# Exponentials split over two PSUM banks each, two projections split by weight halves, a last output piece of 96 columns, and a new timetable

## Chip, cores and metric

One core of a Trainium2 chip. The metric is the device time of one launch in microseconds. The kernel before takes 442.77 us, the median of three runs (442.43 to 443.47). The profiled execution that all rows below come from took 442.87 us; its span, from the first to the last recorded instruction, is 441.1 us, so 1.77 us lie around the span.

## The reference

A transformer block over 2048 tokens of width 576: a memory-augmented attention, then a feed-forward layer, both behind a layernorm and with a residual.

```python
x = A_x                                     # 2048 x 576, bf16
q, k, v = LN(x) @ wq, LN(x) @ wk, LN(x) @ wv  # 32 heads of 18, 4 segments of 512 tokens
for s in range(4):
    p = softmax(q_s k_s^T * 18**-0.5 + causal_mask)      # inside the segment
    a_mem = (phi(q_s) @ M) / (phi(q_s) . z + 1e-6)       # phi(t) = t + 1 if t > 0 else exp(t)
    o_s = g * a_mem + (1 - g) * (p @ v_s)                # g = sigmoid(beta), per head
    M, z = M + phi(k_s)^T v_s, z + sum(phi(k_s))
h = x + concat(o) @ wo
out = h + gelu(LN(h) @ w1 + b1) @ w2 + b2   # hidden width 4608
```

## The kernel before

The program is written as a graph of small steps. `add` makes one step: the engines that may run it and a cost, the function that emits the instructions, the steps it comes after, and the buffers it takes and uses. The order in which steps are emitted, and the engine of each, are not decided at build time: they stand in `TIMETABLE` (line 25), a table from a step's tag and name to a letter (p TensorE, a ScalarE, d VectorE, g GpSimd, s the DMA queue of SyncE) and a rank. `schedule` emits the steps by rank and gives each buffer a slot by a simple model of when slots come free. Each engine then runs its list in order and waits on semaphores for what its next instruction needs.

The tags of the steps: X layernorm and transposing of x, P projections, A attention, M the memory matrix, B output projection and second layernorm, C first and D second feed-forward matmul; the digit is the segment. So A0 is the attention of segment 0. Feed-forward work of one segment is mixed with attention of a later one.

- **PSUM.** `c_s` (line 618) has eight banks of 128 x 512 f32. A width-4 buffer is bank 0 to 3 or 4 to 7. Single-bank buffers prefer banks 4 to 7 where those are free (`pick`, line 357).
- **Scores and exponentials.** One attention step works on four heads: `score` (lines 1020 and 1184) writes four banks by matmuls of 32 rows that run side by side (one bank for each row group), one exponential on ScalarE (lines 1030 and 1192) reads all four banks, 128 x 2048, into `pt`, and masks follow on VectorE or GpSimd (lines 1040, 1043, 1201, 1203). There are 80 such steps, 20 of them in A0. `val` (lines 1059, 1214) multiplies `pt` with v by matmuls of 19 output columns that run side by side.
- **Projections.** `proj2` (line 855, matmuls in line 863) makes k and q of the first two token tiles: two halves of five matmuls of 288 columns, one step of ten. `proj_pair` (line 793) makes the other 60 products, in one of two forms that the ranks decide: where its two steps follow each other directly on TensorE they are emitted as ten matmuls of 128 rows (line 849, called the full form here); where something stands between them, as ten and eight matmuls of 64 rows that run in pairs (line 823, the split form), with a small `pass` memset (line 829) on VectorE or GpSimd between the two halves, for which the second half waits.
- **Layernorm.** `layernorm` (line 733) is two or three VectorE instructions for the statistics (744, 745), two on GpSimd for the root (748, 749), and the apply on VectorE (758 or 760).
- **First loads.** x of tile 0 and 1, then wk as two DMAs of half each, x of tile 2, wq as one DMA of 720 KB, x of tile 3, beta.
- **A0's q and k.** Those of the first 128 tokens are transposed on TensorE (`TQ`, line 906). Those of the others are written to DRAM (`qkd`, line 918) and read back by transposing DMAs (`flip`, line 656) into `qk` and, for tokens 256 to 511, into the tail of `w2_lo` (called w_lo in the profile).
- **The end.** D3 makes 128 x 288 outputs by 36 matmuls each (line 1413); VectorE adds the residual (line 1425), and DMAs write the rows. The last tile is written as two DMAs of half a row each.

Of the kernel before, what the change touches and what calls it, by code (L numbers as in the profile page):

```python
# [335 lines left out]
}  # L336
# [159 lines left out]
def kernel(  # L496
# [12 lines left out]
    P = 128  # L509
# [1065 lines left out]
```

## Time and profile before

| what | value |
|---|---|
| median of three runs | 442.77 us |
| the profiled execution: time, span | 442.87 us, 441.1 us |
| granted TensorE clock | 1.00 over the whole span |
| TensorE busy | 431.6 us, 98% |
| ScalarE, VectorE, GpSimd busy | 297.6, 287.2, 172.7 us |
| 80 exponentials of 128 x 2048 | 150.2 us of ScalarE, 1.88 us each |
| chain that ended last | TensorE 91%, VectorE 3%, ScalarE 2%, DMA 2% |
| first matmul, first projection, last matmul ends | 1.24, 6.93, 438.1 us |

Busy time is the union of an engine's instruction records; matmul ends are modelled, so a busy TensorE can still lose time between matmuls. The chain is read back from the last instruction: each piece is what released the next. Where a row has "idle before" in brackets, the engine stood still for so long, and the name is what ended it.

### The profile page before, as it was taken

Reading aid. Unit: us, or ns where it says so; the run is one execution under the profiler, and the core shown is the slowest. Engines: PE = TensorE matmul, PEld = TensorE weight load, DVE = VectorE, ACT = ScalarE, POOL = GpSimd, SP = SyncE. Lnnn points to the kernel's source line nnn. Section 1 sums busy time; section 2 is a strip of 40 time slices with the busy share of each in tenths; the row PEclk is TensorE's granted clock in tenths of the full one; section 3 lists DMA queues with packets and bytes.
Section 4 is the critical chain, followed back from the end, with each engine's and each line's share of the span. In section 5 each row is a group of like instructions: output and inputs, shape, how many; then the busy total and the mean of one; then the engine's idle time right before and its main releaser. Section 6 shows DMA issues by size and latency. Waiting matters only on the chain.

```text
span 441.1 us, 12208 instructions
## 1 busy us (share of the span) xinstructions
PE 431.6 (98%) x5142; PEld 276.4 (63%) x5142; DVE 287.2 (65%) x651; ACT 297.6 (67%) x270; POOL 172.7 (39%) x317
## 2 busy tenths in 40 slices
PE   7988999999999999999999999999999999999997
PEld 4765677666677677664445666654547775446775
DVE  5999999898878989768899877646875020100002
ACT  3898899999888797777999977653495001656000
POOL 4586678457655434361514576251112010000010
PEclk9999999999999999999999999999999999999999
DMA  6799999988999955981762437924554350650012
GB/s 230 212 235 250 279 294 273 260 196 257 253 226 248 345 119 165 197 222 55 178 194 53 87 106 230 260 57 135 163 192 163 74 129 1 223 180 1 1 28 81
DMA packets 79991, 75.61 MB, mean 171 GB/s; under 512 B 57664, under 2 KB 67264, under 8 KB 79936
## 3 DMA queue, kind: packets, MB, share of 16 engines
q1 hardware_dynamic: 79792, 74.74, 62.6%
q8 instruction: 40, 0.66, 0.6%
q14 instruction: 15, 0.12, 0.1%
q10 hardware_dynamic: 144, 0.09, 0.1%
HBM read 42.30 MB, written 18.87 MB: 139 GB/s over the span
## 4 chain that ended last, share of the span: by engine, by line
PE 91%; DVE 3%; ACT 2%; DMA 2%; issue 1%; POOL 1%; ACTq 0%; DVEq 0%; POOLq 0%
PE bank L1413 33%; PE bank L1326 24%; PE bank L823 8%; PE bank L1363 8%; PE bank L849 5%; PE bank L1188 4%; PE bank L1214 3%; DMA x<-in_A_x_dram 1%; ACT pt L1030 1%; PE bank L1027 1%; PE bank L1059 1%; PE bank L1159 1%; PE bank L953 1%; DMA xnd<-xn 1%; PE bank L772 0%
## 5 line engine op out<-in xcount | busy, mean ns | idle before, releaser
L1413 PEld LDWEIGHTS <-hT 128*128 128x128 bf16 x1152 | 110.0, 98 | 34.7 <-issue 7.2
L1192 ACT ACTIVATE pt<-bank 128x2048 bf16<-128x2048 f32 x60 | 112.6, 1876 | 27.1 <-PE bank L1188 23.6
L1326 PE MATMUL bank<-xreg,w1g 64*128 64x512 bf16 x972 | 107.8, 376 | 0.0
L1326 PEld LDWEIGHTS <-w1g 64*128 64x128 bf16 x972 | 46.6, 94 | 56.4 <-issue 2.9
L1413 PE MATMUL bank<-w_lo,hT 128*128 128x288 bf16 x576 | 77.7, 286 | 0.0
L1413 PE MATMUL bank<-w,hT 128*128 128x288 bf16 x576 | 77.6, 286 | 0.0
L1425 DVE TENSOR_TENSOR ot<-bank,hc 128x288 bf16<-128x288 f32 x32 | 13.8, 451 | 78.1 <-PE bank L1413 70.1
L1331 ACT ACTIVATE hT<-bank,b_col 128x512 bf16<-128x512 f32 x36 | 22.0, 691 | 47.7 <-PE bank L1326 47.5
L1203 POOL TENSOR_SCALAR_AFFINE_SELECT pt<-pt 128x512 bf16<-128x512 bf16 x56 | 38.5, 697 | 26.8 <-ACT pt L1192 26.5
L1341 DVE TENSOR_SCALAR hT<-bank,b_col 128x512 bf16<-128x512 f32 x45 | 32.4, 742 | 16.4 <-PE bank L1326 16.1
L1399 POOL TENSOR_TENSOR hc<-hc,b_bc 128x576 f32<-128x576 f32 x8 | 10.3, 1285 | 77.4 <-DVE ot L1425 59.5
L1030 ACT ACTIVATE pt<-bank 128x2048 bf16<-128x2048 f32 x20 | 37.6, 1879 | 2.6 <-PE bank L1027 1.8
L1363 PE MATMUL bank<-xreg,w1g 64*128 64x256 bf16 x648 | 38.6, 269 | 0.5 <-issue 0.5
L1363 PEld LDWEIGHTS <-w1g 64*128 64x128 bf16 x648 | 30.7, 94 | 6.3 <-issue 2.9
L1346 ACT ACTIVATE hT<-hT 128x8192 bf16<-128x8192 bf16 (+2 forms) x6 | 31.8, 5321 | 0.1
L1339 ACT ACTIVATE hT<-bank,b_col 128x512 bf16<-128x512 f32 x27 | 17.4, 685 | 20.5 <-PE bank L1326 20.4
L823 PE MATMUL bank<-hT,xreg 64*128 64x288 bf16 x414 | 29.1, 283 | 0.6 <-DVE MZacc L963 0.5
L849 PE MATMUL bank<-hT,xreg 128*128 128x288 bf16 x210 | 28.4, 286 | 0.2 <-DVE xreg L669 0.2
L823 PEld LDWEIGHTS <-xreg 64*128 64x128 bf16 x414 | 18.8, 94 | 8.6 <-issue 2.6
L1374 DVE TENSOR_TENSOR hT<-bank,b_col 128x512 bf16<-128x512 f32 x30 | 19.6, 680 | 7.1 <-PE bank L1363 6.9
L1188 PE MATMUL bank<-qk 32*128 32x512 bf16 (+3 forms) x384 | 23.8, 301 | 0.1
L849 PEld LDWEIGHTS <-xreg 128*128 128x128 bf16 x210 | 19.6, 98 | 6.8 <-issue 1.7
(121 smaller groups left out, 590.3 us busy)
## 6 DMA issues: line engine op xcount, KB each, us to landing
w1g<-in_B_w_dram SPq DMA_DIRECT2D x41, 576.0 KB, 5.0
qkd<-qk_pad SPq DMA_DIRECT2D x15, 512.0 KB, 4.1
hd<-h SPq DMA_DIRECT2D x16, 288.0 KB, 4.6
hc<-hd SPq DMA_DIRECT2D x16, 288.0 KB, 3.6
w_lo<-in_B_w_dram SPq DMA_DIRECT2D x3, 864.0 KB, 6.4
w<-in_B_w_dram SPq DMA_DIRECT2D x3, 864.0 KB, 7.9
xb<-in_A_x_dram SPq DMA_DIRECT2D x16, 144.0 KB, 3.7
x2d<-xn SPq DMA_DIRECT2D x14, 160.0 KB, 2.1
```

The lines of the kernel that those rows point to most:

```text
L823: return nc.tensor.matmul(out=cc[hf].t[:, 0:HALF], lhsT=xTb.t[r, k, ts], rhs=wt[r, hf, k, :], start=start, stop=stop, skip_group_check=True)
L849: nc.tensor.matmul(out=cc[hf].t[:, 0:HALF], lhsT=xTb.t[:, k, ts], rhs=wt[:, hf, k, :], start=(k == 0), stop=(k == KT - 1))
L1030: ex = add(ps, {"act": 1.88}, lambda e: nc.scalar.activation(out=pt.t[:], in_=st.t[:], func=ACT.Exp, scale=scale), [sc], pt, [st], table=" ...
L1188: nc.tensor.matmul(out=st.t[:, i, off:off + n_], lhsT=qk[rows, 1, kt * P:(kt + 1) * P], rhs=qk[rows, 0, kt * P:L], start=True, stop=True, ...
L1192: ex = add(ps, {"act": 1.88}, lambda e, st=st, pt=pt: nc.scalar.activation(out=pt.t[:], in_=st.t[:], func=ACT.Exp, scale=scale), [sc], pt, ...
L1203: nc.gpsimd.affine_select(out=blk, in_=blk, pattern=[[0, 4], [1, P]], compare_op=ALU.is_ge, fill=0.0, base=0, channel_multiplier=-1)
L1326: nc.tensor.matmul(out=cc[w].t[:], lhsT=w1.t[rows, k, q, :], rhs=x2T[s].t[rows, k, :], start=(k == 0), stop=(k == ND - 1))
L1331: ready_f[f + w] = [add(pf - 12, {"act": 0.68}, lambda e, f=f, w=w, cc=cc: nc.scalar.activation(out=hT[:, :, f + w, :], in_=cc[w].t[:].rea ...
L1341: nc.vector.tensor_scalar(out=dst, in0=src, scalar1=b, scalar2=None, op0=ALU.add)
L1346: ge = add(2.9, {"act": 0.42 * (f1 - f0) + 0.2}, lambda e, f0=f0, f1=f1: nc.scalar.activation(out=hT[:, :, f0:f1, :], in_=hT[:, :, f0:f1, ...
L1363: nc.tensor.matmul(out=cc[w].t[:, q * 2 * P:(q + 1) * 2 * P], lhsT=w1.t[rows, k, q, :], rhs=x2T[s].t[rows, k, ts], start=(k == 0), stop=(k ...
L1413: nc.tensor.matmul(out=c.t[:, 0:HALF], lhsT=hT[:, tl // 2, f, (tl % 2) * P:(tl % 2 + 1) * P], rhs=w2_c[ch][:, f - ch * WCH, hf * HALF:(hf ...
```

## The change

- **Exponentials.** `exp_of` makes two instructions of 128 x 1024 for each step; each reads a buffer of two banks, which comes free by itself. Masks come after both. A score's four matmuls write two such buffers. `pick` now prefers single banks whose neighbour is taken.
- **First projections.** wq comes as two DMAs of half each; k and q of tiles 0 and 1 become two steps of five matmuls, of which each waits for its weight half alone.
- **Last output half.** The last 288 columns become 192 and 96, each with its own sum, add and DMA.
- **Applies.** A layernorm apply may stand on GpSimd too.
- **Planner constants.** The DMA model (295e3 for 270e3, 1.8 for 1.6) and the order of ranks: all of `TIMETABLE` is new.

```diff
-        return min([i for i in ready if i >= self.home.pref] or ready or range(len(free)), key=lambda i: free[i])
+        return min([i for i in ready if free[i ^ 1] > t0] or ready or range(len(free)), key=lambda i: free[i])
...
-    c_s = Slots([banks_all[:, j, :] for j in range(8)], banks_all, 4)
+    c_s = Slots([banks_all[:, j, :] for j in range(8)], banks_all, 8)
...
-            return add(prio, {"dve": dcost}, apply, [a, b if centred is None else None] + list(extra), dst_buf, [sm, xsrc], name="apply")
+            return add(prio, {"dve": dcost} if centred is not None else {"dve": dcost, "pool": round(dcost + 0.2, 2)}, apply, [a, b if centred is None else None] + list(extra), dst_buf, [sm, xsrc], name="apply")
...
-                        w_ok["q"] = load_w(-7.4, "q", 0)
+                        w_ok["q"] = [load(-7.4 + 0.01 * h, lambda h=h: wts["q"][:, h, :, :].rearrange("p k d -> p (k d)"),
+                                          lambda h=h: A_w[0:P, h * KT * HALF:(h + 1) * KT * HALF], 350e3) for h in range(2)]
...
-            def fn(e):
-                for hf in range(2):
-                    for k in range(KT):
-                        nc.tensor.matmul(out=c.t[:, hf, 0:HALF], lhsT=xTb.t[:, k, ts], rhs=wt[:, hf, k, :],
-                                         start=(k == 0), stop=(k == 4))
-            return add(prio, {"pe": 1.24}, fn, list(after) + w_ok[nm], c, [xTb], name="P" + nm)
+            def fn(e, hf):
+                for k in range(KT):
+                    nc.tensor.matmul(out=c.t[:, hf, 0:HALF], lhsT=xTb.t[:, k, ts], rhs=wt[:, hf, k, :],
+                                     start=(k == 0), stop=(k == 4))
+            a = add(prio, {"pe": 0.62}, lambda e: fn(e, 0), list(after) + w_ok[nm][0:1], c, [xTb], name="P" + nm)
+            return add(prio, {"pe": 0.62}, lambda e: fn(e, 1), list(after) + [a] + w_ok[nm][1:2], None, [c, xTb], name="R" + nm)
...
+        def exp_of(prio, st, pt, sc):
+            ops = []
+            for j in range(2):
+                ops.append(add(prio, {"act": 1.04}, lambda e, j=j: nc.scalar.activation(out=pt.t[:, 2 * j:2 * j + 2, :], in_=st[j].t[:], func=ACT.Exp, scale=scale),
+                               [sc] + ops, [] if j else pt, [st[j]] + ([pt] if j else []), table="exp", name="exp"))
+            return ops
...
-                st, pt = Buf(c_s, width=4), Buf(pt_s)
+                st, pt = [Buf(c_s, width=2), Buf(c_s, width=2)], Buf(pt_s)
...
-                            nc.tensor.matmul(out=st.t[:, i, off:off + n_], lhsT=qk[rows, 1, kt * P:(kt + 1) * P],
+                            nc.tensor.matmul(out=st[i // 2].t[:, i % 2, off:off + n_], lhsT=qk[rows, 1, kt * P:(kt + 1) * P],
...
-                ex = add(ps, {"act": 1.88}, lambda e, st=st, pt=pt: nc.scalar.activation(out=pt.t[:], in_=st.t[:], func=ACT.Exp, scale=scale),
-                         [sc], pt, [st], table="exp", name="exp")
-                exps.append(ex)
+                ex = exp_of(ps, st, pt, sc)
+                exps.extend(ex)
...
+            if s == NSEG - 1:
+                groups[-1:] = [(TPS - 1, 1, HALF, LASTC), (TPS - 1, 2, LASTC, D)]
```

Of the new timetable, by the two programs' lists of instructions in order, engine by engine: of the 60 products of `proj_pair`, 33 stand in the full form (23 before) and 27 in the split form (37 before). TensorE changes between its forms of matmul (128 rows; 64 rows; 32 rows; 19 or 32 output columns) 190 times (205 before). Of the 30 applies that may move, 24 stand on GpSimd, 10 of them for x and 14 for h. The copies of q and k out of PSUM that stand on ScalarE are 26 (31 before). The two-part q of tiles 0 and 1 is ordered: first half of tile 1, first half of tile 0, second half of tile 0, second half of tile 1. The order of the DMA queue is nearly that of before up to the first transposing DMAs of w_lo.

More of the change, by code (lines that the diff above doesn't have):

```diff
@@ L383, in __init__ @@
         d = 0.25 if name == "apply" else 0.14 if name in ("mask", "pq", "comb", "comb2", "memfin", "hc", "fk", "tail", "swap") else 0.0
-        g = 0.15 if name in ("mask", "comb", "comb2", "memfin", "rg", "rk", "hc", "rstd", "eps", "memset", "swap") else 0.0
+        g = 0.15 if name in ("apply", "mask", "comb", "comb2", "memfin", "rg", "rk", "hc", "rstd", "eps", "memset", "swap") else 0.0
         self.rest = (round(cost["dve"] - d, 4) if d and "dve" in cost else 0.0, round(cost["pool"] - g, 4) if g and "pool" in cost else 0.0)
@@ L476, in schedule @@
             if e == "sp":
-                dma = max(dma, op.end) + op.size / 270e3
-                op.end = dma + 1.6
+                dma = max(dma, op.end) + op.size / 295e3
+                op.end = dma + 1.8
                 flying.append(op.end)
@@ L532 @@
     ND = 9
+    LASTC = 480
     DIRECT = 3
@@ L784, in stage_X @@
                     if tl == 1:
-                        w_ok["q"] = load_w(-7.4, "q", 0)
+                        w_ok["q"] = [load(-7.4 + 0.01 * h, lambda h=h: wts["q"][:, h, :, :].rearrange("p k d -> p (k d)"),
+                                          lambda h=h: A_w[0:P, h * KT * HALF:(h + 1) * KT * HALF], 350e3) for h in range(2)]
                         xs_pre.append(load_x(-7.3, 2))
                         xs_pre.append(load_x(-7.2, 3, xs_pre[2][0]))
-                        for op in (xs_pre[2][1], xs_pre[3][1], w_ok["q"][0]):
+                        for op in (xs_pre[2][1], xs_pre[3][1], w_ok["q"][0], w_ok["q"][1]):
                             held(op).after.append(x_gate)
@@ L1015, in step @@
                 n += 1
-                st, pt, masks, deps = Buf(c_s, width=4), Buf(pt_s), {}, []
+                st, pt, masks, deps = [Buf(c_s, width=2), Buf(c_s, width=2)], Buf(pt_s), {}, []
                 lb = [lo_b[2 * Q], lo_b[2 * Q + 1]]
@@ L1026, in score @@
                             rows = slice(32 * i, 32 * i + 32)
-                            nc.tensor.matmul(out=st.t[:, i, off:off + n_], lhsT=kk[rows, 4 * Q + b, 1, ks],
+                            nc.tensor.matmul(out=st[i // 2].t[:, i % 2, off:off + n_], lhsT=kk[rows, 4 * Q + b, 1, ks],
                                              rhs=qq[rows, 4 * Q + b, 0, qs], start=True, stop=True, tile_position=(32 * i, 0))
                 sc = add(ps, {"pe": 0.28 if len(units) > 2 else 0.24}, score, deps, st, lb, table="rows32", name="st0")
-                ex = add(ps, {"act": 1.88}, lambda e: nc.scalar.activation(out=pt.t[:], in_=st.t[:], func=ACT.Exp, scale=scale),
-                         [sc], pt, [st], table="exp", name="exp")
-                exps.append(ex)
+                ex = exp_of(ps, st, pt, sc)
+                exps.extend(ex)
                 diag = [u for u in units if u[1] * P == u[2]]
@@ L1044, in mask @@
                                                     base=0, channel_multiplier=-1)
-                    masks[u] = add(ps, {"dve": 0.87, "pool": 1.17}, mask, [ex, tri_ok], None, [pt], name="mask")
+                    masks[u] = add(ps, {"dve": 0.87, "pool": 1.17}, mask, [*ex, tri_ok], None, [pt], name="mask")
                     masks[u].bias = {"dve": MASK_BIAS}
-                return [(4 * Q + b, kt, q0, n_, off, pt) for (b, kt, q0, n_, off) in units], [ex] + list(masks.values())
+                return [(4 * Q + b, kt, q0, n_, off, pt) for (b, kt, q0, n_, off) in units], ex + list(masks.values())
             def values(tag, t0, parts, banks, acq, cost):
@@ L1191, in stage_A @@
                 sc = add(ps, {"pe": 0.23}, score, [qk_ok[g] for g in gs], st, [qks[g] for g in gs], table="rows32", name="st")
-                ex = add(ps, {"act": 1.88}, lambda e, st=st, pt=pt: nc.scalar.activation(out=pt.t[:], in_=st.t[:], func=ACT.Exp, scale=scale),
-                         [sc], pt, [st], table="exp", name="exp")
-                exps.append(ex)
+                ex = exp_of(ps, st, pt, sc)
+                exps.extend(ex)
                 for (dg, kt, off, n_) in step:
@@ L1204, in mask @@
                                                     base=0, channel_multiplier=-1)
-                    mk = add(ps, {"dve": 0.45, "pool": 0.67}, mask, [ex] + later, None, [pt], name="mask")
+                    mk = add(ps, {"dve": 0.45, "pool": 0.67}, mask, [*ex, *later], None, [pt], name="mask")
                     mk.bias = {"dve": MASK_BIAS}
@@ L1388, in stage_C @@
                     f1_last[half] = a
-            groups = [(tl, hf) for tl in range(TPS) for hf in range(2)]
+            groups = [(tl, hf, hf * HALF, (hf + 1) * HALF) for tl in range(TPS) for hf in range(2)]
+            if s == NSEG - 1:
+                groups[-1:] = [(TPS - 1, 1, HALF, LASTC), (TPS - 1, 2, LASTC, D)]
             hcs, ots, lasts = {}, {}, {}
-            for gi, (tl, hf) in enumerate(groups):
+            for gi, (tl, hf, c0, c1) in enumerate(groups):
                 gr.tag = f"D{s}{tl // 2 if s == 0 else ''}"
@@ L1409, in stage_C, with fn @@
                     ch = n if up else NF // WCH - 1 - n
-                    def fn(e, c=c, ch=ch, n=n, tl=tl, hf=hf):
+                    def fn(e, c=c, ch=ch, n=n, tl=tl, c0=c0, c1=c1):
                         for f in range(ch * WCH, (ch + 1) * WCH):
-                            nc.tensor.matmul(out=c.t[:, 0:HALF], lhsT=hT[:, tl // 2, f, (tl % 2) * P:(tl % 2 + 1) * P],
-                                             rhs=w2_c[ch][:, f - ch * WCH, hf * HALF:(hf + 1) * HALF], start=(n == 0 and f == ch * WCH), stop=(n == NF // WCH - 1 and f == (ch + 1) * WCH - 1))
+                            nc.tensor.matmul(out=c.t[:, 0:c1 - c0], lhsT=hT[:, tl // 2, f, (tl % 2) * P:(tl % 2 + 1) * P],
+                                             rhs=w2_c[ch][:, f - ch * WCH, c0:c1], start=(n == 0 and f == ch * WCH), stop=(n == NF // WCH - 1 and f == (ch + 1) * WCH - 1))
                     pp = prio + 0.5 + (0.001 * n + 0.0001 * gi if gi < 2 else 0.05 * gi)
                     deps = [prev, w2_ok[ch], f1_last[tl // 2]] + [ready_f.get(f) or ready_f[f, tl // 2] for f in range(ch * WCH, (ch + 1) * WCH)]
+                    fc = round(0.015 + 0.0025 * (c1 - c0), 4)
                     if prev is None:
-                        v = add(pp, {"pe": 0.735}, fn, deps, [c, tk], name="F2")
+                        v = add(pp, {"pe": fc}, fn, deps, [c, tk], name="F2")
                     else:
-                        v = add(pp, {"pe": 0.735}, fn, deps, None, [c, tk], name="F2")
+                        v = add(pp, {"pe": fc}, fn, deps, None, [c, tk], name="F2")
                     prev = v
@@ L1423, in stage_C @@
                         f2_chunks.setdefault((s, f), []).append(v)
-                cs = slice(hf * HALF, (hf + 1) * HALF)
-                o = add(p2 - 16, {"dve": 0.46}, lambda e, cs=cs, c=c, ot=ot, hc=hc: nc.vector.tensor_tensor(
-                    out=ot.t[:, cs], in0=c.t[:, 0:HALF], in1=hc.t[:, cs], op=ALU.add), [prev, hc.op] + ([lasts[tl]] if hf else []),
+                cs = slice(c0, c1)
+                o = add(p2 - 16, {"dve": round(0.16 + 0.00104 * (c1 - c0), 2)}, lambda e, cs=cs, c=c, ot=ot, hc=hc: nc.vector.tensor_tensor(
+                    out=ot.t[:, cs], in0=c.t[:, 0:cs.stop - cs.start], in1=hc.t[:, cs], op=ALU.add), [prev, hc.op] + ([lasts[tl]] if hf else []),
                     ot if hf == 0 else None, [c, hc] + ([] if hf == 0 else [ot]), name="oadd")
@@ L1429, in stage_C @@
                 if s == NSEG - 1 and tl == TPS - 1:
-                    load(p2 - 10, lambda t=t, cs=cs: of[t * P:(t + 1) * P, cs], lambda ot=ot, cs=cs: ot.t[:, cs], 74e3, [o], use=[ot])
+                    load(p2 - 10, lambda t=t, cs=cs: of[t * P:(t + 1) * P, cs], lambda ot=ot, cs=cs: ot.t[:, cs], 256 * (c1 - c0), [o], use=[ot])
                 elif hf == 1:
```

623 rows, old and new, of the table TIMETABLE are left out of this document.

## Prediction, made before the result was known

> **What bounds the kernel now.** I read the 40 slices and the chain first, then engine time by stage, then TensorE's own waits, then the rows where those waits end.
>
> ```profile
> PE   7988999999999999999999999999999999999997
> DVE  5999999898878989768899877646875020100002
> ACT  3898899999888797777999977653495001656000
> ...
> PE 91%; DVE 3%; ACT 2%; DMA 2%; issue 1%; POOL 1%; ACTq 0%; DVEq 0%; POOLq 0%
> ```
>
> TensorE is busy in nearly every tenth after the first few slices, and the chain is TensorE for 91%. Where it is busy, only fewer matmuls or fewer breaks between them shorten the run. The stages (in order: us, then busy time of TensorE, its weight loads, VectorE, ScalarE, GpSimd, then clock and DMA):
>
> ```profile
> core 0: us, PE busy (x) PEld busy (x) DVE busy (x) ACT busy (x) POOL busy (x), PEclk, DMA share, GB/s
> 17.20:43.08 25.88, 22.44 (x411) 15.89 (x409) 24.87 (x62) 23.96 (x31) 19.34 (x34) 1.00 0.89 230
> 43.08:120.00 76.92, 76.37 (x1241) 53.67 (x1241) 68.65 (x171) 72.72 (x70) 50.82 (x113) 1.00 1.01 257
> 120.00:300.00 180.00, 179.91 (x2131) 109.53 (x2125) 142.89 (x308) 143.48 (x102) 83.85 (x130) 1.00 0.66 171
> 300.00:438.15 138.15, 138.11 (x1253) 87.78 (x1248) 38.73 (x82) 48.50 (x55) 10.75 (x19) 1.00 0.35 109
> ```
>
> From 43.08 to 438.15 TensorE stands still for 0.68 us in 395 (0.55 + 0.09 + 0.04). From 17.20 to 43.08 it stands still for 3.44 us of 25.88, and there VectorE (24.87) and ScalarE (23.96) are nearly full. So waits can be won in one stage only, and at the two ends. TensorE's waits up to 44 us:
>
> ```profile
> PE bank L1027 <- ACT pt L1030: 1.8, 3, 1.0
> PE bank L823 <- DVE MZacc L963: 0.5, 1, 0.5
> PE bank L863 <- DMA hT<-in_A_w_dram: 0.4, 1, 0.4
> ```
>
> The rows of that stage:
>
> ```profile
> 20.08 1.88 ACT L1030 ACTIVATE pt<-bank 128x2048 bf16<-128x2048 f32 x1
> ...
> 21.85 0.39 ACT L665 CAST qk_pad<-bank 128x288 bf16<-128x288 f32 x1
> ...
> 24.22 0.36 SPq L918 DMA_DIRECT2D qkd<-qk_pad  x1
> ...
> 29.31 2.58 SPq L656 DMA_TRANSPOSE w_lo<-qkd  x2
> ...
> 34.33 0.12 PEld L1027 LDWEIGHTS <-qk 32*128 32x128 bf16 x8 [0.85 <-DMA w_lo<-qkd]
> ...
> 36.77 0.40 PE L1027 MATMUL bank<-w_lo 32*128 32x128 bf16 x16 [0.61 <-ACT pt L1030]
> ...
> 40.76 2.06 PE L823 MATMUL bank<-hT,xreg 64*128 64x288 bf16 x26 [0.49 <-DVE MZacc L963]
> ...
> 43.08 2.13 PE L849 MATMUL bank<-wt_o,oT 128*128 128x288 bf16 x16
> ```
>
> Three things are read here. Scores (L1027) wait for the exponential before them, which frees its four banks only at its end. The DMA chain from the last store of q and k (24.22) over the transposing DMAs (29.31) to the first score of tokens 256 and on (34.33) takes 10.11 us. And 43.08, where the output projection of tile 0 starts, closes the stage.
>
> **The change, part by part.** All against the profiled execution (442.87 us, span 441.1); the median of the runs shown lies 0.10 below it.
>
> *Breaks on TensorE.* The price of a change of matmul form comes from the chain:
>
> ```profile
> 89.03 6.73 PE bank L823 x108
> ...
> 115.34 2.56 PE bank L849 x20
> ...
> 148.91 2.31 PE bank L1413 x18
> 151.54 2.31 PE bank L1413 x18
> ```
>
> 288 matmuls of 288 columns take 35.39 us in the chain's longest D2 piece, 0.123 each, so 18 take 2.21. The row at 148.91 has 2.31: 0.10 for the change behind it. The score between the two rows takes 151.54 - 151.22 = 0.32, of which 512 columns at 0.123/288 us each are 0.22: again 0.10. 205 changes become 190: 15 x 0.10 = 1.5 us less.
>
> *Projections.* A product in split form costs 6.73/6 = 1.12 us (row 89.03), in full form 10 x 0.123 = 1.23 (2.56/2 = 1.28 with its drain, row 115.34). Ten more in full form: 10 x 0.11 = 1.1 more, at most 10 x 0.16 = 1.6.
>
> *Last half in two.* Columns stay; 36 matmuls are added. The 16 matmuls of 76 columns at 34.66 took 0.66 us, 0.041 each against 0.032 for their columns: 0.009 x 36 = 0.3 more. TensorE's work in all: -1.5 + 1.1 + 0.3 = -0.1.
>
> *The tail.* After the last matmul comes an add of 288 columns (0.46) and a DMA (441.10 - 438.61 = 2.49). An add of 96 columns lies between 0.24 (128x16, L1226) and 0.45 (128x288, L1425): 0.30 by the line through both. The DMA carries a third; its time is mostly latency (2.5 median for this tensor, 1.6 shortest), so I take 0.1 off, between 0 and 0.9. Sum -0.25.
>
> *The first k and q.* The page gives TensorE a wait of 0.4 for wq. With halves it goes, but the next step is late anyway: in ScalarE's new list the small exponential of beta (L1466) stands ahead of both copies of q, and beta landed 6.8 us after its issue at 4.86, so at 11.66. The copy of tile 0's q can then start at 11.88, is done at 12.62, and the transposes that need it started at 12.59 before. Worth 0.0. GpSimd makes the identity after the memset of one pad and the mark that waits for x (3.34), so at 3.34 + 0.18 + 0.85 + 0.20 + 0.29 = 4.86; tile 0's transposes can start then (5.60 before), but those of tile 1 stand ahead of the first k and wait for their apply (6.2): k starts at 6.65 instead of 6.93, and that is lost again at 11.66.
>
> *The exponentials.* No row is 128x1024 exp. The nearest: a ScalarE copy from PSUM of that shape, 1.01; half of 128x2048, 0.94; the line through 128x512 gelu (0.69) and 128x2048 (1.88), 1.085. I take 1.02. ScalarE's instructions overlap where nothing waits: 20.08 + 1.88 = 21.96, yet the next row starts at 21.85, 0.11 earlier. A pair is then 1.02 + 1.02 - 0.10 = 1.94, +0.06 each: 9 x 0.06 = 0.5 before 43.08, 23 x 0.06 = 1.4 from there to 120, where ScalarE has 76.92 - 72.72 = 4.2 free. Between the first exponential and the tenth, ScalarE's new list sums to 23.1 us by the rows of before (each less 0.10 for the overlap), the old one to 23.5; it took 26.0 (17.2 to 43.2). So ScalarE can run up to 2.5 us earlier there, if it is fed.
>
> *The stage to 43.08, step by step in the new order.* ScalarE from 11.66: the beta row, four copies and a memset for tile 0 and 1 (0.22, 0.74, 0.74, 0.39, 1.01, 1.01), three copies and an ek (1.20, 0.68), each less 0.10, and 0.3 of waiting for the transposes: first exponential at 17.0 (17.2 before). q of tile 2 stands behind six more copies and one ek on ScalarE: its store leaves at 24.65 (24.22 before): 17.0, four half exponentials 4.08, five copies of v 2.24, four of k and q 1.60, ek 0.68, less 14 x 0.10, and 0.45 of waiting for the second score and v. The chain of 10.11 us then ends at 34.75, so the first score of the upper tokens is 0.4 later, with 0.5 us more of matmuls done ahead of it: a draw. From there the waits at 36.77 (0.61, banks) and 40.76 (0.49, then 0.43 for the `pass`) have no place: a score needs two pairs of four, and the products there are in full form. Scores and values of the second half then end at 36.6, the two transposes, two reciprocals, two products, a swap and three transposes on VectorE (0.7 + 0.7, 0.5, 0.4, 0.5, 0.9, 0.2, 1.2 with overlaps) end at 41.9, against 42.4. The output projection starts at 42.0 instead of 43.08. Two applies instead of nine are left to VectorE there, which is its cover; without it 7 x 0.45 = 3 us would return. I take 0.9 less, between 0 and 2.5.
>
> *From 43 to 438.* 24 applies go from VectorE (0.55 and 0.71) to GpSimd; nobody on TensorE waited for them. Scores stand within 3 us of their old places in TensorE's list until the last. I take 0, between -0.6 (the one wait at 82.3) and +3.
>
> Sum: -0.1 - 0.25 - 0.9 = -1.25; 442.87 - 1.25 = 441.6, less 0.10 for the median: **441.5**.
>
> **Rivals.**
>
> *ScalarE becomes the bound (slower).* Place: 43.08 to 120, 23 exponentials, 4.2 us free. It decides from 4.2/23 = 0.18 more per exponential, a pair of 2.06. At 1.085 without overlap a pair is 2.17, +0.29: 6.7 - 4.2 = 2.5 us late, and the 0.9 is gone too: 442.8 - 0.35 + 2.5 = 445.0. For it: no two exponentials ran back to back in this trace. Against: other ScalarE pairs overlap by 0.10. The Trainium skill, ScalarE: Activation LUTs, Rules for kernel authors, budgets about 0.3 us per ACTIVATE and 0.83 ns per element, which speaks against splitting: 1.15 each, 2.30 a pair, as an estimate. By that estimate the time would be 442.4 + 23 x 0.42 - 4.2 = 448. The row of 1.88 for 128x2048, where the page's rule gives 2.0, and the overlap speak for less.
>
> *GpSimd is late (slower).* Up to 43.08 it is busy 19.34 of 25.88 and takes six applies of 640 columns: at 0.78 (from 0.70 for 576, L927) 4.7, fits; at 1.43 (from 1.285, two f32 inputs, L1399) 8.6, 2 us over. Besides, L748 took 0.71 at 20.25 while VectorE's L929 ran and 0.22 alone at 21.94. Then 442.4 + 2 = 444.4. The Trainium skill, SBUF — State Buffer, Who interferes with whom, has VectorE and GpSimd lock out each other on a shared port pair; the two L748 rows agree.
>
> *The start stays as it was.* The upper DMA chain or the oT chain takes what the pairs give: 442.77 - 0.35 = 442.4, no change.
>
> *All waits of the stage go (faster).* 3.44 idle, 0.9 counted: 2.5 more, 439.0. Against it stands the DMA chain, which the change does not shorten.
>
> **How the numbers follow.** Forecast 0.50, of which 0.12 ends within 0.2% (0.9 us, about what a measurement of this kernel tells from no change); all waits gone 0.10; start unchanged 0.12; ScalarE 0.14; GpSimd 0.14, of which 0.02 is too small to tell. Faster 0.38 + 0.10 = 0.48, same 0.12 + 0.12 + 0.02 = 0.26, slower 0.26. The range reaches from all waits gone (439.0) to the ScalarE case (445.0), with 0.4 on either side for the tail and the stage from 43 to 438; the page's 448 lies outside.
>
> **What would show it.** Right: 128x1024 rows at about 1.02 us, starting 0.1 before the end of the one ahead; first upper score near 34.8 and the output projection near 42; no wait of TensorE for L1027's exponential over 0.3; last matmul near 437. Wrong: exponential rows over 1.03 or gaps inside a pair; TensorE waits of over 1 us after 43; GpSimd applies over 1 us, with VectorE or the xnd stores waiting for them; a start of the output projection after 43.

## Result: 461.2 us, 4.1% slower

The changed kernel takes 461.24 us, the median of six runs (459.10 to 462.48), against 442.71 for the kernel before beside it (442.43 to 444.30). The ratio is 1.041, with a 95% interval of 1.038 to 1.044. The forecast was 441.5, and the range ended at 445.4. The profiled execution took 462.2 us with a span of 460.5, so 19.4 more than the span of 441.1 before.

The page of the changed kernel, slices and chain:

```profile
PE   8858898989799999989999999999999999999997
...
POOL 4899999948953774964444296434105600000000
PEclk9998999999989999999999999999999999999999
...
PE 67%; POOL 22%; DMA 4%; issue 2%; DVE 2%; SPq 1%; POOLq 0%
```

GpSimd, which carried 1% of the chain, now carries 22%, and it is full in slices 3 to 8. The stages of the prediction, with the same columns (us, then busy time of TensorE, its weight loads, VectorE, ScalarE, GpSimd, then clock and DMA):

```profile
17.20:43.08 25.88, 19.45 (x335) 14.16 (x324) 17.71 (x43) 18.96 (x31) 24.73 (x33) 0.93 0.65 172
43.08:120.00 76.92, 70.32 (x1080) 50.99 (x1078) 63.96 (x158) 65.04 (x76) 65.50 (x110) 1.00 0.97 248
120.00:300.00 180.00, 174.03 (x2096) 107.45 (x2094) 129.49 (x290) 145.63 (x152) 105.60 (x150) 0.99 0.64 173
```

GpSimd is busy 24.73 us of 25.88 in the first of these (19.34 before), while VectorE and ScalarE, both nearly full before, have become slack (17.71 and 18.96). TensorE stands still for 6.43 us there (3.44 before), for 6.60 in the second stage (0.55) and for 5.97 in the third (0.09).

The 19.4 us divide as follows. Up to its last matmul (457.18, before 438.12) TensorE idles 22.7 us instead of 6.5: 16.2 more. It is busy 434.47 instead of 431.60: 2.9 more, to which the last section comes back. The tail behind the last matmul is 3.32 instead of 2.98: 0.3.

What TensorE waited for, from its list of waits (total us, times, longest):

```profile
PE bank L1072 <- POOL pt L1056: 6.4, 2, 4.6
PE bank L830 <- POOL mark_pool L836: 5.4, 3, 3.0
PE bank L1201 <- DMA qk<-qkd: 1.7, 1, 1.7
PE bank L913 <- ACT qk_pad L669: 1.5, 1, 1.5
```

Two kinds of waits on GpSimd, for a mask (line 1056) and for the mark of a `pass` (line 836), make 11.8 us. Neither instruction is slow. The timeline shows what stands ahead of them in GpSimd's list, at the longest wait and at the one after 122 us:

```profile
28.14 5.55 POOL L766 TENSOR_SCALAR xn<-x,ln 128x640 bf16<-128x640 bf16 x2
33.67 0.66 POOL L934 TENSOR_SCALAR rk<-qk_pad 128x576 bf16<-128x576 bf16 x1
34.29 1.10 POOL L1056 TENSOR_SCALAR_AFFINE_SELECT pt<-pt 128x1024 bf16<-128x1024 bf16 x1
...
35.45 0.61 PE L1072 MATMUL bank<-pt,v_aug 128*19 128x128 bf16 x16 [4.63 <-POOL pt L1056]
...
121.87 2.41 POOL L766 TENSOR_SCALAR xn<-h,ln 128x576 bf16<-128x576 f32 x1
...
125.97 0.54 PE L830 MATMUL bank<-hT,xreg 64*128 64x288 bf16 x6 [3.03 <-POOL mark_pool L836]
```

Two applies (line 766) hold GpSimd for 5.55 us. The exponential whose mask comes behind them was done by 30.9 at the latest: ScalarE's last pair before it started at 28.96 and took 1.94. At the later wait four more instructions of 0.23 to 0.67 us stand between the apply and the mark. The groups of the page give the price of an apply (count, then busy us and mean ns of one):

```profile
L766 POOL TENSOR_SCALAR xn<-h,ln 128x576 bf16<-128x576 f32 x14 | 33.5, 2395 | 0.9
...
L766 POOL TENSOR_SCALAR xn<-x,ln 128x640 bf16<-128x640 bf16 x10 | 25.7, 2573 | 0.8
```

On VectorE these were 0.55 to 0.71; the prediction had 0.78 to 1.43 for them on GpSimd. They take 2.40 and 2.57, 59.2 us in all.

### The profile page after: what moved, and what is told of

Read it like the earlier page. It is cut to its first block, busy times and chain, and to the rows that moved or that the text cites. A ratio compares the mean times of both kernels' runs of the same rounds, so it can differ in the third digit from the quotient of the medians.

```text
span 460.5 us, 12247 instructions
## 1 busy us (share of the span) xinstructions
PE 434.5 (94%) x5101; PEld 280.5 (61%) x5101; DVE 270.8 (59%) x622; ACT 301.3 (65%) x345; POOL 230.5 (50%) x341
## 4 chain that ended last, share of the span: by engine, by line
PE 67%; POOL 22%; DMA 4%; issue 2%; DVE 2%; SPq 1%; POOLq 0%
PE bank L1427 25%; PE bank L1338 23%; POOL xn L766 10%; PE bank L1375 6%; PE bank L830 5%; PE bank L1201 3%; POOL pt L1056 3%; PE bank L1226 2%; POOL ln L755 2%; DMA x<-in_A_x_dram 2%; POOL ln L754 1%; POOL rk L934 1%; SPq L655 1%; DMA qk<-qkd 1%; DMA w1g<-in_B_w_dram 1%
## 5 line engine op out<-in xcount | busy, mean ns | idle before, releaser
L990 ACT ACTIVATE pt<-bank 128x1024 bf16<-128x1024 f32 x160 | 155.2, 1024 | 42.6 <-PE bank L1201 18.6
L1427 PE MATMUL bank<-w,hT 128*128 128x288 bf16 (+2 forms) x594 | 78.5, 283 | 0.0
L1427 PE MATMUL bank<-w_lo,hT 128*128 128x288 bf16 (+2 forms) x594 | 78.3, 283 | 0.0
L1440 DVE TENSOR_TENSOR ot<-bank,hc 128x288 bf16<-128x288 f32 (+2 forms) x33 | 14.2, 443 | 70.4 <-PE bank L1427 64.9
L1215 POOL TENSOR_SCALAR_AFFINE_SELECT pt<-pt 128x512 bf16<-128x512 bf16 x59 | 38.0, 657 | 30.6 <-ACT pt L990 30.4
L856 PE MATMUL bank<-hT,xreg 128*128 128x288 bf16 x290 | 39.8, 291 | 0.1
L766 POOL TENSOR_SCALAR xn<-h,ln 128x576 bf16<-128x576 f32 x14 | 33.5, 2395 | 0.9
L856 PEld LDWEIGHTS <-xreg 128*128 128x128 bf16 x290 | 27.5, 99 | 9.3 <-issue 2.1
L1245 POOL TENSOR_TENSOR o_nat<-t,t 128x288 bf16<-128x288 f32 x16 | 16.6, 1035 | 22.5 <-DVE t L1187 11.5
L830 PE MATMUL bank<-hT,xreg 64*128 64x288 bf16 x270 | 19.5, 292 | 7.2 <-POOL mark_pool L836 5.4
L766 POOL TENSOR_SCALAR xn<-x,ln 128x640 bf16<-128x640 bf16 x10 | 25.7, 2573 | 0.8
```

Of the source, the lines that this page charges most:

```text
L766: VEC[e].tensor_scalar(out=dst_buf.t[:, 0:w], in0=src(), scalar1=sm.t[:, 12:13], scalar2=sm.t[:, 15:16], op0=ALU.subtract, op1=ALU.mult)
L830: return nc.tensor.matmul(out=cc[hf].t[:, 0:HALF], lhsT=xTb.t[r, k, ts], rhs=wt[r, hf, k, :], start=start, stop=stop, skip_group_check=True)
L856: nc.tensor.matmul(out=cc[hf].t[:, 0:HALF], lhsT=xTb.t[:, k, ts], rhs=wt[:, hf, k, :], start=(k == 0), stop=(k == KT - 1))
L990: ops.append(add(prio, {"act": 1.04}, lambda e, j=j: nc.scalar.activation(out=pt.t[:, 2 * j:2 * j + 2, :], in_=st[j].t[:], func=ACT.Exp, s ...
L1215: nc.gpsimd.affine_select(out=blk, in_=blk, pattern=[[0, 4], [1, P]], compare_op=ALU.is_ge, fill=0.0, base=0, channel_multiplier=-1)
L1427: nc.tensor.matmul(out=c.t[:, 0:c1 - c0], lhsT=hT[:, tl // 2, f, (tl % 2) * P:(tl % 2 + 1) * P], rhs=w2_c[ch][:, f - ch * WCH, c0:c1], sta ...
```

## Experiments

Three theories. A: the duration of an apply on GpSimd is the only wrong term, and the loss is what queues behind it. B: GpSimd is slow because VectorE works beside it. C and D: the new order and the two-bank buffers make the waits themselves, wholly (C) or in part, at the start (D). Later expectations name rivals of their own, and use the letter D for others too. Ratios are against the kernel before, run on the same chip in the same session.

### The price of the apply by itself

**probe_forms**: ten instructions behind the last one of GpSimd in the kernel before; the number behind each is its line in the trace.

```diff
+        nc.gpsimd.tensor_scalar(out=out16, in0=src[:], scalar1=mean, scalar2=rs, op0=ALU.subtract, op1=ALU.mult)   # 1513
+        nc.gpsimd.tensor_scalar(out=out16, in0=src[:], scalar1=0.5, scalar2=2.0, op0=ALU.subtract, op1=ALU.mult)   # 1514
+        nc.gpsimd.tensor_scalar(out=out16, in0=src[:], scalar1=2.0, scalar2=0.5, op0=ALU.min, op1=ALU.max)         # 1515
+        nc.gpsimd.tensor_scalar(out=out16, in0=src[:], scalar1=mean, scalar2=None, op0=ALU.subtract)               # 1516
...
+        nc.gpsimd.tensor_tensor(out=out16, in0=src[:], in1=rs.to_broadcast([P, D]), op=ALU.mult)                   # 1522
```

> The kernel before with ten more GpSimd instructions behind its last one, on tiles that are dead by then; their results go nowhere, and the time of the whole is not what is looked at. All have 128x576 elements but one of 128x288. The apply's form, (x - column) * column from f32 to bf16, took 2.30 us as a rule in the changed kernel. Theory A, GpSimd's own price for that form: 2.3 again here, though VectorE has almost nothing to do. Theory B, VectorE's traffic beside it made it slow: about 0.7 here, the row of GpSimd's min/max on 128x576 bf16. Within A: if the columns are what costs, the same with two constants takes 0.7 and one column alone about 1.5 (half way); if the subtract and multiply cost, both forms take 2.3 and min/max with constants 0.7.

GpSimd's timeline (start, us, instruction):

```profile
421.13 2.31 POOL L1513 TENSOR_SCALAR xn<-h,ln 128x576 bf16<-128x576 f32 x1
423.53 2.15 POOL L1514 TENSOR_SCALAR xn<-h 128x576 bf16<-128x576 f32 x1
425.76 0.67 POOL L1515 TENSOR_SCALAR xn<-h 128x576 bf16<-128x576 f32 x1
426.53 1.73 POOL L1516 TENSOR_SCALAR xn<-h,ln 128x576 bf16<-128x576 f32 x1
...
436.49 1.15 POOL L1522 TENSOR_TENSOR xn<-h,ln 128x576 bf16<-128x576 f32 x1
```

The apply's form takes 2.31 where VectorE is nearly idle, as in the middle of the kernel (shortest 2.297). B falls. The columns cost little (2.15 without them); the pair of operations does: min and max take 0.67 on the same elements.

### Taking the applies off GpSimd

**all_dve**, **x_dve**: the changed kernel, its buffers and order, with the applies (in x_dve those of the first layernorm alone) issued on VectorE.

```diff
-            op.fn(op.eng)
+            op.fn("dve" if op.name == "apply" else op.eng)                            # all_dve
+            op.fn("dve" if op.name == "apply" and op.tag[0] == "X" else op.eng)       # x_dve
```

> The changed kernel with the 24 applies back on VectorE, at the place where they stand in the written order; banks, splits and the order of all else are those of the changed kernel. Theory A, GpSimd's slow applies hold up the masks, marks and rk rows behind them: nearly all of the 18.5 us go, 440 to 445, and no wait of TensorE over 1.5 us is left, nor a granted clock under 0.9. Rival C, the new order and the narrower banks make the waits: 455 or more, with the waits for the masks and marks still there.

> The changed kernel with only the ten applies of the first LayerNorm (640 columns) back on VectorE; 14 of the second stay on GpSimd. Up to 120 us TensorE was busy 10.3 us less in the changed kernel than before (103.3 against 113.6), and most applies there are of the first LayerNorm; behind 120 about 6 us, all beside applies of the second. Theory A: 449 to 454, with the waits at 30.6, 77.7 and 98.5 gone and those at 122.7 and 203.6 left. Rival C: 455 or more.

all_dve: 445.66 (444.24 to 448.07), ratio 1.005 (1.003 to 1.007). No wait for a mask or a mark on GpSimd over 0.2 us is left, and 15.6 of the 18.5 us are gone: C falls. It is just over the 445 that A allowed. Two more of A's signs failed: in its profile, which is of the slowest of the six runs, TensorE waited 1.9 us for a transposing DMA (w_lo), and the clock was at 0.51 for 3.4 us (0.93 over the stage from 17 to 43). So a part is left to explain.

x_dve: 452.28, ratio 1.021 (1.018 to 1.023), inside A's 449 to 454. The wait at 30.6 is gone, the long one for the mark stays (it ends at 116.6 here):

```profile
PE bank L830 <- POOL mark_pool L836: 3.6, 2, 3.0
```

Taken off in this order, the first layernorm's ten applies are worth 9.0 us and the second's fourteen 6.6.

**before_pool**: the kernel before, with the same 24 applies issued on GpSimd and nothing else changed.

> The kernel before with the same 24 applies issued on GpSimd, each at its place in the old order, and nothing else changed. Theory A: the applies alone make it slow, 452 to 465, with a GpSimd busy time near 230 us. Rival C: the applies are hidden as the costs in the program assume, at most 1% over the kernel before (447).

468.81, ratio 1.059 (1.056 to 1.061), beyond A's upper end: the applies alone cost 26 us in an order written without them, more than the whole change. About 9 of these are not waiting but slower work: TensorE is busy 440.7 us instead of 431.6, with the clock at half for six stretches of 3.4 us (last section). The same two waits lead its list:

```profile
PE bank L823 <- POOL mark_pool L829: 10.2, 4, 4.3
PE bank L1059 <- POOL pt L1043: 5.2, 1, 5.2
```

### The changed kernel with the price that was predicted

**fast_apply**: the changed kernel with nothing moved; only the operations of GpSimd's applies differ, and so the duration (this kernel leaves the layernorm out of 24 tiles).

```diff
-                VEC[e].tensor_scalar(..., op0=ALU.subtract, op1=ALU.mult)
+                o0, o1 = (ALU.min, ALU.max) if e == "pool" else (ALU.subtract, ALU.mult)
+                VEC[e].tensor_scalar(..., op0=o0, op1=o1)
```

> The changed kernel, with nothing moved, but the 24 applies on GpSimd take minimum and maximum in place of subtract and multiply, with the same two columns: the LayerNorm is left out of them, and only the duration of the instruction changes. Min/max with constants took 0.67 us on 128x576 in the probe, so I expect 0.7 to 0.9 here, about what the prediction had put in. Theory A (the price of the apply was the only wrong term): 440 to 443, the predicted 441.5 within it. Theory D (the new order loses at the start too, as the 445.7 with all applies on VectorE hints): 444 to 447, with TensorE's waits before 43 us still there.

440.68 (439.71 to 441.39), ratio 0.994 (0.992 to 0.996), inside A's 440 to 443 and 0.8 under the forecast. The applies took 0.82 and 0.87 as medians. D falls for this order as it is written. Its stages, and from its timeline the output projection that closed the first of them before:

```profile
17.20:43.08 25.88, 23.91 (x405) 17.53 (x403) 23.52 (x60) 24.48 (x39) 23.73 (x38) 1.00 0.99 223
43.08:120.00 76.92, 76.76 (x1218) 56.30 (x1218) 68.19 (x164) 69.90 (x84) 57.74 (x122) 1.00 1.03 269
120.00:300.00 180.00, 180.00 (x2097) 109.26 (x2095) 134.23 (x296) 146.69 (x150) 89.47 (x137) 1.00 0.61 167
```

```profile
40.64 2.62 PE L857 MATMUL bank<-wt_o,oT 128*128 128x288 bf16 x20
```

From 43.08 on TensorE idles 0.16 us up to 300; the output projection starts at 40.64 (43.08 before, 49.14 in the changed kernel).

**apply_tt**: a price in between; GpSimd's apply is a subtract of the mean only, on two tensors.

```diff
+                if e == "pool":
+                    nc.gpsimd.tensor_tensor(out=dst_buf.t[:, 0:w], in0=src(), in1=sm.t[:, 12:13].to_broadcast([P, w]), op=ALU.subtract)
+                    return
```

> The changed kernel with the 24 applies on GpSimd as a subtract of the mean only, as an operation on two tensors (the mean spread over the row): 1.15 to 1.4 us each by the probe; the multiply by the rstd is left out. It puts the price between fast_apply (0.82 to 0.87, 440.7 us) and the changed kernel (2.3 to 2.5, 461.2). Along the straight line between these, 20.5 us over 1.55, it would be 445 to 447. The prediction's own case of a late GpSimd had 444.4 at 1.43. If GpSimd's time is slack up to some price, as it has 2 us free of 26 to 43 us and more behind, 441 to 443.

443.42, ratio 1.002 (1.001 to 1.003), below the straight line and 0.4 above the case of slack. The medians were 1.15 and 1.25. From 0.84 to 1.20 us (means of the two medians) the run grows by 2.7 us, 7.6 per us of price; from 1.20 to 2.41 by 17.8, 14.7 per us. Neither stretch is flat; what lies under 0.84 was not tried.

### The rest of the change

**before_exp2**: the kernel before, each exponential as two instructions at the old place.

```diff
-lambda e: nc.scalar.activation(out=pt.t[:], in_=st.t[:], func=ACT.Exp, scale=scale)
+lambda e: [nc.scalar.activation(out=pt.t[:, j:j + 2, :], in_=st.t[:, j:j + 2, :], func=ACT.Exp, scale=scale) for j in (0, 2)]
```

> The kernel before with each exponential issued as two instructions on two banks each, one right behind the other, at the place of the old one; order, banks and engines of all else are the old ones. The prediction's terms: a pair 1.94 for 1.88, and the waits of TensorE for the exponential (1.8 us in three waits before) shrink because the first two banks come free a microsecond earlier: 441.5 to 443, no difference that can be told from none or a small gain. Rival (ScalarE as the bound from 43 to 120 us): 445 or more, pairs over 2.06.

443.39, ratio 1.001 (0.999 to 1.002). Splitting alone, with the order and the four-bank buffers kept, brings nothing and costs nothing that can be told; TensorE's wait for the exponential only shrinks from 1.8 to 1.4 us. The gain of fast_apply lies in the rest of the change with it (order, two-bank buffers, split weights); these were not taken apart.

**all_dve2**: all_dve with three applies and a root moved in the order of issue.

```diff
+        op.rank = {45: 57.5, 144: 131.1, 148: 131.2, 149: 131.3}.get(op.start, op.start)
...
-    order = build().schedule()
+    order = sorted(build().schedule(), key=lambda o: o.rank)
```

> The kernel all_dve with three of the applies and one rstd moved in VectorE's list: the apply of tile 2 stands behind the copy of tile 1's transposes instead of ahead of it (TensorE had waited 1.3 us for that copy at 15.2), and two applies of segment 1 stand ahead of two copies instead of ahead of the masks (TensorE had waited 0.9 for a mask at 31.8, and the stores behind them on SP 2 us later for the upper score). Theory E (what is left in all_dve comes from places that were written for GpSimd): 442 to 444. Theory D (it comes from the rest of the new order, the row of beta on ScalarE above all): 445 to 446.

445.26, ratio 1.004 (1.001 to 1.006): D's number and not E's 442 to 444. On VectorE the applies cost some 4.6 us more than at 0.82 to 0.87 on GpSimd, wherever these three stand. TensorE's busy time up to 17 us is 14.55 in its profile against 15.67 in fast_apply, and from 17 to 43 it is 22.38 against 24.03; which step loses it was not taken further apart.

### A cheap form of the apply

**probe_ops**: ten more forms behind the kernel before.

```diff
+        nc.gpsimd.tensor_scalar(out=out16, in0=src[:], scalar1=rs, scalar2=mean, op0=ALU.mult, op1=ALU.add)        # 1513
+        nc.gpsimd.tensor_scalar(out=out16, in0=src[:], scalar1=mean, scalar2=rs, op0=ALU.min, op1=ALU.max)         # 1514
+        nc.gpsimd.tensor_scalar(out=out16, in0=src[:], scalar1=mean, scalar2=rs, op0=ALU.min, op1=ALU.mult)        # 1515
+        nc.gpsimd.tensor_scalar(out=out16, in0=src[:], scalar1=mean, scalar2=None, op0=ALU.add)                    # 1516
+        nc.gpsimd.tensor_scalar(out=out16, in0=src[:], scalar1=mean, scalar2=None, op0=ALU.max)                    # 1517
```

> The kernel before with ten other GpSimd instructions of 128x576 behind its last one; their results go nowhere. The first probe had 2.31 for subtract and multiply by columns, 1.73 for one of them, 0.67 for min/max with constants, 1.15 for a product of two tensors, one of them a column spread over the row. If the kind of operation sets the price: multiply and add 2.3, min/max with columns 0.8 (0.82 in fast_apply), min and multiply between 1.2 and 2.0, add alone 1.7, max alone 0.7, and the tensor subtract 1.15. If only subtract and multiply are slow, multiply and add comes out under 2. A form of the whole LayerNorm at under 1 us would make a faster kernel possible.

```profile
421.82 0.81 POOL L1513 TENSOR_SCALAR xn<-h,ln 128x576 bf16<-128x576 f32 x1
422.74 0.82 POOL L1514 TENSOR_SCALAR xn<-h,ln 128x576 bf16<-128x576 f32 x1
423.65 2.31 POOL L1515 TENSOR_SCALAR xn<-h,ln 128x576 bf16<-128x576 f32 x1
426.06 1.75 POOL L1516 TENSOR_SCALAR xn<-h,ln 128x576 bf16<-128x576 f32 x1
427.91 1.72 POOL L1517 TENSOR_SCALAR xn<-h,ln 128x576 bf16<-128x576 f32 x1
```

My guess on the kind of operation was wrong: multiply and add take 0.81, while min and multiply take 2.31, and a single max 1.72, more than the pair of min and max. Of the forms tried, two pairs are cheap, and every other pair and single operation of this instruction is dear. A layernorm can be written in the cheap pair, as x * rstd + (-mean * rstd).

**mult_add** and **before_pool_ma**: that form for GpSimd's applies, in the changed kernel and in before_pool.

```diff
+                if e == "pool":
+                    nc.gpsimd.tensor_scalar(out=sm.t[:, 14:15], in0=sm.t[:, 12:13], scalar1=sm.t[:, 15:16], scalar2=-1.0, op0=ALU.mult, op1=ALU.mult)
+                    nc.gpsimd.tensor_scalar(out=dst_buf.t[:, 0:w], in0=src(), scalar1=sm.t[:, 15:16], scalar2=sm.t[:, 14:15], op0=ALU.mult, op1=ALU.add)
+                    return
```

> The changed kernel with the 24 applies on GpSimd written as x * rstd + (-mean * rstd): a product of 128x1 for the second column, then one multiply and add over the row. The whole LayerNorm is computed. The probe had 0.81 us for multiply and add on 128x576; with 0.2 to 0.3 for the small product an apply costs 1.05 to 1.2. Theory A (the price of an apply on GpSimd is the term that was wrong): between fast_apply (0.82 to 0.87, 440.7) and apply_tt (1.15 to 1.25, 443.4): 441.5 to 443.4, at or a little under the kernel before. Theory D (the gain of fast_apply came from the values it left out, not from the time): 445 or more.

> The kernel before with the same 24 applies on GpSimd in the multiply-and-add form, in the old order (before_pool took 468.8 with subtract and multiply). Theory A: nearly all of that loss goes, 443 to 447; the old order has the applies in places written for VectorE, so some of GpSimd's masks and marks come late. If the new order is worth nothing, it is as fast as mult_add.

mult_add: 444.60, ratio 1.004 (1.002 to 1.006), 16.6 us less than the changed kernel but 1.2 above the expected range, and just under the 445 of the rival by which fast_apply gained from the values it left out; the small product took 0.26, the row 0.82 or 0.87. The next run speaks against that rival. before_pool_ma: 451.47, ratio 1.017 (1.014 to 1.019), above its 443 to 447. In the old order even cheap applies on GpSimd cost 8 us, so the rest of the change (order, two-bank buffers, splits) is worth 6.9 us once the applies are there.

**eps_dve**: mult_add, and the add of epsilon moved to VectorE behind the variance.

```diff
                 nc.vector.bn_aggr(out=sm.t[:, 12:14], ...)
+                nc.vector.tensor_scalar(out=sm.t[:, 14:15], in0=sm.t[:, 13:14], scalar1=EPS, scalar2=None, op0=ALU.add)
-                nc.gpsimd.tensor_scalar(out=sm.t[:, 14:15], in0=sm.t[:, 13:14], scalar1=EPS, scalar2=None, op0=ALU.add)
```

(The small product then goes to column 13.)

> The kernel mult_add, with the add of epsilon to the variance (32 instructions of 128x1, 0.23 us each on GpSimd in its trace) moved to VectorE, right behind the instruction that makes the variance, where a 128x1 fill takes 0.06. GpSimd's list then holds one small instruction and one row per apply and a single power in front: 0.23 + 0.07 of issue less per LayerNorm than mult_add, about what fast_apply has, with the whole LayerNorm computed. Theory A (what counts is GpSimd's time in the first 120 us): 440.5 to 443, below mult_add's 444.6 and perhaps below the kernel before. Theory F (the second hop between instructions of one apply costs, or VectorE's 32 more instructions do): 444 or more.

441.79 (441.26 to 442.92), ratio 0.996 (0.995 to 0.997): faster than the kernel before by 0.4%, and than the changed kernel by 19 us, with the whole layernorm computed. GpSimd's list at the place where the changed kernel stood for 5.55 us (start, us):

```profile
24.37 0.88 POOL L768 TENSOR_SCALAR xn<-x,ln 128x640 bf16<-128x640 bf16 x1
...
26.08 0.87 POOL L768 TENSOR_SCALAR xn<-x,ln 128x640 bf16<-128x640 bf16 x1
27.04 0.67 POOL L938 TENSOR_SCALAR rk<-qk_pad 128x576 bf16<-128x576 bf16 x1
27.67 1.10 POOL L1060 TENSOR_SCALAR_AFFINE_SELECT pt<-pt 128x1024 bf16<-128x1024 bf16 x1
```

The mask (line 1056 in the changed kernel, 1060 here) starts at 27.67 instead of 34.29.

## Why the prediction was wrong

**The step that failed** is the term of the applies, in two places. In the rival "GpSimd is late" an apply was priced at 0.78 (from the row of L927) to 1.43 (from L1399). The first row is a min and max, one of the two cheap pairs, the second an operation on two tensors; neither is the apply's form, and the nearest row in elements was taken for the nearest in kind. It measured 2.52 as the median on 640 columns, so the six applies that it put up to 43.08 are 15.1 us instead of 4.7 to 8.6, where 6.5 us were free; only four of them had started by then. In the stage from 43 to 438 the prediction said that nobody on TensorE waited for the applies, and took 0, at most 3. That sentence is true and beside the point: TensorE waits for the masks and marks that stand behind them in the same list. It lost 11.9 us there. The rival had the mechanism right, and its 444.4 at the upper price was about right for that price: from apply_tt (443.4 at 1.20) the two slopes give 444.6 to 445.8 at 1.36, the mean of its 1.285 and 1.43, as an estimate. Its price was too low, and it was given one stage only. Its second reason, VectorE working beside GpSimd, is not what made the apply slow (probe_forms). The range therefore ended 16 us short.

The Trainium skill, GPSIMD Engine Reference, 3.1 Elementwise, gives 1.8 cycles per element at best and 2.6 with two inputs; at its 1.2 GHz that would be 0.86 and 1.25 us for 576, as an estimate. The rows of 0.81 and 1.15 lie 6 and 8% under these, the 0.67 of min and max with constants a fifth under the best case; the 2.31 of the apply's form, 4.8 such cycles, lies far above both, and the runs decide.

**The other steps**, read in fast_apply, where the price was the predicted one:

- TensorE's work: 431.35 us busy against 431.60, predicted -0.1. Right as a sum; its three parts were not measured apart.
- Exponentials: the 160 rows average 1.024 (predicted 1.02), pairs 1.94. ScalarE is busy 69.90 of 76.92 from 43.08 to 120; the ScalarE rival did not come. Right.
- The first k and q were put at 0.0, since beta would land at 11.66 and hold ScalarE. In the changed kernel it landed at 12.5 and did: TensorE waited 1.5 us for the copy of q behind it (line 913), and the first exponential started at 17.39 (17.0 predicted). Up to 17.20 TensorE was busy 13.49 us instead of 14.77, a loss of 1.3. In fast_apply beta landed by 10.5, q followed TensorE, and the first exponential started at 15.73: TensorE was busy 15.87, a gain of 1.1 that the sum did not have. The landing of one small DMA weighs on this term, but does not decide it alone: in x_dve ScalarE took beta at 10.82, and the first exponential still started at 17.25.
- The stage from 17.20 to 43.08: 1.97 us of standing instead of 3.44, so 1.5 less where 0.9 was taken (0 to 2.5), and the first upper score at 32.60 where 34.75 was forecast; a part of that comes from the earlier start. Right in kind, a little small.
- The tail, -0.25: last matmul to end took 3.19 us (438.0 - 434.81) against 2.98. The add shrank from 0.46 to 0.26 as forecast; the DMA of a third of the bytes took 2.89, not less than the 2.49 before. The changed kernel had 3.32 in all and all_dve 2.76, so the term is 0 within 0.3.

Of what was said would show it wrong, three signs came in the changed kernel: GpSimd applies over 1 us, with VectorE waiting for them (xn at line 1283, 5.8 us in four waits); TensorE waits over 1 us after 43; and an output projection that started after 43, at 49.14.

## What to carry to other kernels

Before work is moved to another engine, its price there must come from the same instruction with the same operations; where no row has that, the upper bound has to be wide, or a probe behind the last instruction, which costs one run, has to give it. Here the moved work was paid by what stands behind it in the list of its new engine, more than by those who wait for its result. And a slow form may have a cheap twin: writing the same layernorm as multiply and add turned a loss of 4.1% into one of 0.4%, and with the add of epsilon moved besides into a gain of 0.4%.

## What was not expected of the hardware

**Pairs of operations.** GpSimd's 128x576 row takes 0.81 us for multiply and add, 0.67 to 0.82 for min and max, but 2.31 for subtract and multiply or min and multiply, and 1.7 for any single operation tried.

**The clock answers to standing still.** After the two longest waits the granted clock was 0.50 for 3.4 us. The stretches below are 3.4 us long (columns as above, the clock third from the end), two of the changed kernel's pairs and one of all_dve:

```profile
31.60:35.00 3.40, 0.00 (x0) 0.00 (x0) 0.00 (x0) 0.00 (x0) 3.40 (x3) 1.00 0.26 93
35.00:38.40 3.40, 2.95 (x40) 1.88 (x40) 2.19 (x4) 1.70 (x2) 3.18 (x6) 0.50 0.91 257
123.80:127.20 3.40, 1.23 (x20) 0.82 (x24) 0.01 (x1) 0.45 (x2) 3.40 (x9) 0.99 0.25 93
127.20:130.60 3.40, 3.40 (x40) 1.62 (x34) 2.06 (x5) 2.59 (x4) 1.46 (x3) 0.50 0.91 267
```

```profile
35.90:39.30 3.40, 1.54 (x61) 1.14 (x60) 2.84 (x6) 1.63 (x3) 3.14 (x7) 1.00 1.33 122
39.30:42.70 3.40, 3.40 (x58) 2.10 (x46) 3.33 (x11) 2.98 (x4) 1.68 (x4) 0.51 1.12 344
```

The two dips of the changed kernel begin 92.2 us apart (35.0 and 127.2), 27 times 3.41, which fits a fixed grid of 3.41 us. The trace of before_pool bears it out: there the half clock sets in at 29.11, 46.17, 66.66 and 83.72, which is 5, 6 and 5 times 3.41 apart, and it lasts one or two such lengths. Cut along the grid (each trace along its own dips), the stretches at full clock with TensorE busy for 0.00 to 1.55 us were followed by a dip, eight in the changed kernel, all_dve, before_pool and before_pool_ma; those with 1.58, 1.75, 1.89 and more were not. So it counts where the grid cuts a wait: in before_pool_ma one of 2.06 us, which ended at 55.17, lay in one stretch (busy for 1.35) and brought a dip, while one of 2.41, which ended at 40.59, was cut in two (busy for 2.50 and 1.91) and brought none.

A dip of 3.4 us costs at most 1.7 us. In its two dips the changed kernel's TensorE was busy for 2.95 and 3.40 us; half of that, 3.2, is near the 2.9 us more of busy time than before, and the 3.1 more than in fast_apply, which without a dip has the same matmuls in 431.35. Busy time has other causes too: all_dve2, also with the same matmuls and no dip, has 433.09. The Trainium skill, TensorE: Matmul & The Clock Gate, Part 1, has half the clock after an idle window of about 3.4 us until a busy one has passed. The lengths agree with the rows; the window need not be idle, as the stretches with 1.23 and 1.54 us of work show.

The clock also differs between runs of one kernel: four of mult_add's twelve runs have a mean clock of 1.000 and took 443.24 to 444.30, the eight at 0.996 took 444.40 to 446.75. 0.4% of 442 us is 1.8, about one dip as an estimate, so this is likely a part of what put it above its expected range. Of all_dve's six runs only the one of 448.07 has a clock under 1.000 (0.995); the spread of the others, 444.24 to 446.27, stays open.
